# A new hand-written order for an attention and feed-forward kernel, with one small cast moved

## The chip, the cores and the metric

The kernel runs on one core of a Trainium2 chip. The metric is the device time of one launch in microseconds (us), and lower is better. The core's engines work side by side, each through its own queue of instructions in order: PE (TensorE, the matmuls), DVE (VectorE), ACT (ScalarE), POOL (GpSimd) and SP (SyncE, which here only issues DMAs and small waits). PSUM holds matmul results in 8 banks of 512 f32 columns; all other data lie in SBUF.

## The reference

Two branches share the input x (2048 tokens, 640 columns, bf16), and a gate per token mixes them:

```
g = sigmoid((x * gate_w).sum(-1))
q, k, v = x @ wqkv                     # 32 heads of 20 columns
p = softmax(q k^T * 20**-0.5)          # 2048 x 2048 for each head
a = (p v, heads joined) @ wo
h = x @ w1 + b1                        # 1536 columns
b = (h * tanh(softplus(h))) @ w2       # "mish"
out = g * a + (1 - g) * b
```

The bulk of it is the 32 x 2048 x 2048 exponentials, and the score and value matmuls around them.

## The kernel before

**Tiling.** Four heads form a quad (8 of them), and 512 queries a chunk (4 of them); a quad and a chunk make a group, 32 groups G in all. A group has 16 key tiles of 128 keys. A *unit* is the scores of one head, one key tile and one chunk: 128 x 512, one PSUM bank. The four heads of a quad lie 32 rows apart, so up to four score matmuls (L1119), each of 32 rows, can run in PE side by side: a *run* of scores is row-tiled. Everything else on PE is column-tiled: four matmuls of 32 or 21 columns side by side make one *column round*, four value products (L1154, "PV", into the accumulating bank) or one *piece* of a dense product (L699).

**Two ways to the exponential.** Most units go to ACT: one ACTIVATE (L1137) takes one, two or three neighbouring banks and writes into the ring E. The rest, 668 units, go to DVE: L615 (`power_of`) writes the integer whose bits are 2 to the score, into a tile T of four units (one key tile of a group). Such a tile is corrected by POOL: `add_shift` (L645) adds a constant to 64-bit words. `d_take` sets how. With `two` at 0, POOL makes two shifted copies and PV takes the tile in three column rounds. With `two` at 1, POOL makes one copy, DVE adds the two tiles (`total`, L669, 128 x 2048), POOL shifts the other copy, and PV needs two rounds.

**Normalising.** When a group's PV is complete, DVE transposes the bank (L1183), takes reciprocals (L1190) and multiplies by them (L1197, from two SBUF inputs, T1 and rec, into T2), and SP stores the result. L669 and L1197 are the operations with two inputs in SBUF that matter in what follows.

**The dense work.** Every dense product is a *chain* of pieces into one bank and a copy by DVE at its end: keys and queries (`dense_chain`, weights `ws`, stored by way of `st`), values, the hidden product (`h_chain`, weights `w1t`; its copy, L882, adds the bias b1f and writes `big`), its second half (`b_chain`, from `big` and `w2_sb`) and the output product (`wo_chain`; its copy, L998, reads `bl`, a part loaded back from HBM by `load_b`, L965, into one of three slots, which come free when the copies of an earlier `bl` are through). Pieces of the hidden, key and query products are 512 columns wide, those of `b_chain` and `wo_chain` 320. A piece can also be split in four *row parts* (L688), each riding in a run of scores with fewer than four units; SP then issues a small wait (L695) between the parts.

**What sets the order.** The string ORDER, some 6200 tokens, is read from left to right, and each token emits instructions: `S n,bank` n units of scores; `x n` an ACTIVATE over n banks; `D G,j,r,bank` one score unit for DVE, whose L615 waits in a list; `d G,k,two` sets a key tile of group G aside for DVE; `y n` emits the nth waiting DVE operation; `p n,tag` the nth waiting POOL addition; `V j,i` a column round of PV; `C` begins a chain and `F` emits its next piece; `f chain,row` emits one row part. Loads have letters of their own (`l` calls `load_late`). Each engine then runs its share in that order.

**The cast.** The bias b1 is loaded as bf16 (b1bf) by `load_late(2)`. The copy of the very first hidden chain casts it to f32 (L881) just ahead of its own addition.

Of the kernel before, what the change touches and what calls it, by code (L numbers as in the profile page):

```python
# [19 lines left out]
S2,5 x2 S2,2 S2,0 C0,4 C1,5 C2,6 F0 F0 F0 F0 F0 F1 y1 F y3 x2 C3,5 S1,2 y4 S1,3 C4,6 x2 x2 F3 F S1,0 y5 S1,1  # L20
C6,5 F F d1,2,0 F F y2 F d0,0,0 x2 F S1,3 y6 x1 S1,2 S1,4 F F F F x1 C5,6 F6 F6 F6 F F6 F F F F6 F6 x1 F6 C7,0
F6 F6 F6 C8,4 y7 S3,1 x2 F7 F5 F7 F7 y8 y9 F7 F F7 y10 y12 S2,1 x1 y11 S2,5 V1,-1 F F F F C9,3 d1,7,0 V0,-1 F8
F8 F8 y13 F8 F8 x2 F F8 F8 F8 F8 S3,0 F8 F8 F8 F8 x2 F8 F8 F x3 F F y14 F S2,5 V2,-1 x2 V3,-1 S1,0 y15 S1,1
y16 y17 C11,5 S1,2 y18 y19 S2,3 C10,6 x3 V4,-1 F F11 F11 F11 F11 F11 F11 F F F11 F F S1,1 q1 S1,2 V5,-1 x2 F11
F11 y20 v0,0 F11 F11 F11 F11 S1,0 C12,3 x2 S1,4 D0,15,3,6 F11 F11 F11 F11 F11 x1 F11 F F11 x1 F y23 S2,1
D0,15,0,0 y24 d3,4,0 d0,6,0 y25 y26 y27 F y28 x2 D0,15,2,5 S1,4 y29 S1,6 F V6,-1 F x1 y30 x1 l3 y31 S1,0 S1,2
x1 C13,5 F F S1,6 x1 S1,3 D0,14,3,1 S1,4 C14,0 F13 F x1 F F13 F13 F y32 y33 F F F V7,-1 S2,1 D0,15,1,6 y34 F F
F F x2 F F F F D0,14,0,5 S2,3 V8,-1 F F y35 F F F x2 D0,14,1,6 S2,1 y36 F V9,-1 C15,6 y37 y38 y39 x2 V10,-1
S3,3 x2 F F y40 F x3 F y41 l2 F F F F D0,14,2,2 y22 S2,0 y21 p1,8 V15,0 F F V11,-1 S1,5 y42 S1,3 y43 V14,0 y44
D1,15,1,2 x2 S1,4 S1,0 p2,-1 y45 S1,1 x1 p3,-1 C16,5 D1,15,0,6 V12,-1 F F V15,1 F y46 x2 F F l0 x2 F F d2,3,0  # L30
S3,2 D1,15,2,6 F p4,5 V15,2 F y47 F V13,-1 S2,0 x3 D1,14,0,6 V14,2 V14,1 y48 y49 S1,3 y50 y51 C17,5 D1,15,3,2
# [306 lines left out]
def kernel(  # L338
# [1106 lines left out]
```

## Time and profile before

| what | value |
|---|---|
| time, median of 3 runs | 685.02 us (684.34 to 685.22) |
| the profiled execution's own time | 685.2 us |
| its span | 683.4 us, so 1.8 us lie around the span |
| busy: PE, ACT, DVE, POOL | 674.0, 667.9, 603.0, 356.8 us |
| granted TensorE clock | 9 tenths or more in all 40 slices, mean 1.00 from 10 to 674 us |

In the profile, a group of instructions is told by its line, engine, operation and tile; its columns are the summed busy time, the mean duration of one, and the idle time of the engine just ahead of them with what ended it. A row of the timeline has the start, the length, the engine and line, and in brackets how long the engine stood idle before it and for what. Matmuls that overlap have overlapping rows, so on PE the distance between starts says more than the length.

### The profile page before, as it was taken

To read this page: it belongs to the slowest core of one execution; us is meant where nothing else is said; L and a number is where in the kernel's file an instruction comes from. 1 tells how busy PE (TensorE), PEld (TensorE's weight loads), DVE (VectorE), ACT (ScalarE), POOL (GpSimd) and SP (SyncE) were. 2 spreads that over 40 slices of the span, in tenths; PEclk is the share of its full clock that TensorE was granted. 3 is DMA by queue.
4 is the path that set the end of the run, shared out by engine and by line. 5 is a ranking of instruction groups with operands and counts; after the bars stand their busy time and mean duration, and the time that the engine had idled before them with its cause. 6 is when DMAs were issued, how large, how long until landed. Compare 5 with 4: busy or idle time off the path is not lost.

```text
span 683.4 us, 24492 instructions
## 1 busy us (share of the span) xinstructions
PE 674.0 (99%) x10339; PEld 236.7 (35%) x10339; DVE 603.0 (88%) x1037; ACT 667.9 (98%) x695; POOL 356.8 (52%) x349
## 2 busy tenths in 40 slices
PE   8999999999999999999999999999999999999997
PEld 4433332323333443333333223222243333333333
DVE  5688989899999889999889988999998988899896
ACT  6999999999999999999999999999999999999995
POOL 5045555454454535575555545456645655565543
PEclk9999999999999999999999999999999999999999
DMA  7443422214312121112132113321322113162231
GB/s 170 99 100 94 89 49 71 49 34 93 74 25 53 38 48 27 26 39 38 44 92 42 34 58 89 46 70 28 58 55 73 19 30 64 25 82 43 56 86 59
DMA packets 128542, 40.47 MB, mean 59 GB/s; under 512 B 94960, under 2 KB 127872, under 8 KB 128432
## 3 DMA queue, kind: packets, MB, share of 16 engines
q1 hardware_dynamic: 126032, 38.29, 25.5%
q8 instruction: 81, 1.33, 0.8%
q10 hardware_dynamic: 2400, 0.62, 0.4%
q14 instruction: 29, 0.24, 0.1%
HBM read 22.29 MB, written 12.78 MB: 51 GB/s over the span
## 4 chain that ended last, share of the span: by engine, by line
PE 81%; ACT 12%; DVE 3%; issue 3%; DMA 1%; POOL 0%; SPq 0%; DVEq 0%; POOLq 0%; ACTq 0%
PE Sp L699 27%; PE Sp L1119 26%; PE Sp L1154 26%; ACT E L1137 12%; DVE T L615 1%; DMA wf<-in_A_wqkv_dram 1%; PE Sp L688 0%; DVE T L669 0%; DVE st L784 0%; DVE T L1197 0%; POOL T L645 0%; PE Sp L1384 0%; PE Sp L1169 0%; DVE ot L1401 0%; PE Sp L1263 0%
## 5 line engine op out<-in xcount | busy, mean ns | idle before, releaser
L1137 ACT ACTIVATE E<-Sp 128x1024 bf16<-128x1024 f32 (+2 forms) x677 | 635.9, 1090 | 3.5 <-PE Sp L1119 2.7
L645 POOL INT64_ADD T<-T x334 | 347.0, 1050 | 311.7 <-DVE T L615 180.1
L615 DVE TENSOR_SCALAR T<-Sp 128x512 int16<-128x512 f32 x668 | 438.1, 684 | 49.8 <-PE Sp L1119 41.0
L1119 PE MATMUL Sp<-qT,kT 32*128 32x512 bf16 x2048 | 260.9, 383 | 1.9 <-DVE T L615 0.9
L1119 PEld LDWEIGHTS <-kT 32*128 32x128 bf16 x2048 | 69.5, 91 | 234.1 <-issue 229.2
L1154 PE MATMUL Sp<-E,VA 128*21 128x512 bf16 x1380 | 129.5, 382 | 0.0
L1154 PE MATMUL Sp<-T,VD 128*21 128x512 bf16 x1272 | 117.6, 382 | 0.1
L699 PE MATMUL Sp<-w_sb,big 128*32 128x320 bf16 x1508 | 77.1, 302 | 0.3 <-DVE T L615 0.2
L699 PE MATMUL Sp<-xT,w1t 128*32 128x512 bf16 x952 | 75.0, 382 | 0.0
L1154 PEld LDWEIGHTS <-VA 128*21 128x21 bf16 x2048 | 44.8, 90 | 62.8 <-issue 55.5
L1154 PE MATMUL Sp<-T,VA 128*21 128x512 bf16 x668 | 64.1, 382 | 0.0
L699 PE MATMUL Sp<-xT,ws 128*32 128x512 bf16 x720 | 56.6, 382 | 0.3 <-DVE VA L838 0.2
L699 PEld LDWEIGHTS <-big 128*32 128x32 bf16 x1508 | 34.0, 95 | 30.3 <-issue 21.2
L1154 PEld LDWEIGHTS <-VD 128*21 128x21 bf16 x1272 | 31.1, 90 | 36.8 <-issue 29.8
L882 DVE TENSOR_SCALAR big<-Sp,b1f 128x512 bf16<-128x512 f32 x48 | 35.6, 742 | 2.2 <-PE Sp L699 1.8
L699 PE MATMUL Sp<-wv,xT 128*32 128x81 bf16 (+2 forms) x960 | 34.8, 257 | 0.0
L699 PE MATMUL Sp<-wo_sb,od 128*32 128x320 bf16 (+1 forms) x604 | 30.3, 300 | 0.0
L699 PEld LDWEIGHTS <-w1t 128*32 128x32 bf16 x952 | 21.5, 94 | 25.2 <-issue 18.0
L784 DVE CAST st<-Sp 128x512 bf16<-128x512 f32 x36 | 24.4, 684 | 2.8 <-PE Sp L699 2.1
L1183 DVE STREAM_TRANSPOSE T<-Sp 128x512 f32<-128x512 f32 x32 | 22.7, 709 | 2.2 <-PE Sp L1154 2.0
L699 PEld LDWEIGHTS <-xT 128*32 128x32 bf16 x960 | 20.6, 96 | 11.3 <-issue 5.9
L699 PEld LDWEIGHTS <-ws 128*32 128x32 bf16 x720 | 17.1, 95 | 19.1 <-issue 12.5
(82 smaller groups left out, 222.5 us busy)
## 6 DMA issues: line engine op xcount, KB each, us to landing
w1t<-in_B_w_dram SPq DMA_DIRECT2D x24, 320.0 KB
q_dram<-st SPq DMA_DIRECT2D x20, 128.0 KB
b_dram<-bt SPq DMA_DIRECT2D x16, 160.0 KB
bl<-b_dram SPq DMA_DIRECT2D x16, 160.0 KB
qT<-q_dram SPq DMA_DIRECT2D x124, 20.0 KB
o_dram<-T SPq DMA_DIRECT2D x120, 20.0 KB
out_dram<-ot SPq DMA_DIRECT2D x15, 160.0 KB
kT<-k_dram SPq DMA_DIRECT2D x28, 80.0 KB
```

The lines of the kernel that those rows point to most:

```text
L615: nc.vector.tensor_scalar(out=dst.bitcast(I16), in0=src, scalar1=inv_sqrt_dh * LOG2E * 128.0, scalar2=127.0 * 128.0 + (BETA2 if two else B ...
L645: nc.gpsimd.int64_add(dst[:, :].bitcast(I64), src[:, :].bitcast(I64), n * 0x0001000100010001)
L699: nc.tensor.matmul(out_[k : k + 32], lhsT=lhsT[:, k : k + 32], rhs=rhs, tile_position=(0, k), start=start, stop=ch.done(), skip_group_chec ...
L784: nc.vector.tensor_copy(out=res["st"][:, :], in_=ps[:, :])
L882: nc.vector.tensor_scalar(out=big[:, pair_of(c, ft), (ft % 2) * QC : (ft % 2 + 1) * QC], in0=ps[:, :], scalar1=b1f[:, ft : ft + 1], scalar ...
L1119: nc.tensor.matmul(ps_cols, lhsT=kT[p][32 * t_ : 32 * t_ + 32, j * P : (j + 1) * P], rhs=qT[G][32 * t_ : 32 * t_ + 32, :], tile_position=( ...
L1137: nc.scalar.activation(E[:, x : x + n, :], allb[:, k0 : k0 + n, :], ACT.Exp, scale=inv_sqrt_dh,)
L1154: nc.tensor.matmul(acc[32 * t_ : 32 * t_ + DH + 1, :], lhsT=lhsT, rhs=rhs, start=(pv_done[G] == 0), stop=(pv_done[G] == pv_total[G] - 1), ...
L1183: nc.vector.transpose(out=st["T1"][:, :, :].rearrange("p b r -> p (b r)"), in_=acc[:, :])
```

## The change

The whole string ORDER is replaced by another one, and the cast of b1 becomes an operation of its own on the list of waiting DVE operations, entered by `load_late(2)` right after the DMA of b1 is issued. In the new kernel lines move up or down by one: L615 is L616, L645 L646, L669 L670, L699 L700, and from the deleted lines on L1119 is L1118, L1154 L1153, L1197 L1196, L998 L997, L965 L964.

```diff
-S2,5 x2 S2,2 S2,0 C0,4 C1,5 C2,6 F0 F0 F0 F0 F0 F1 y1 F y3 x2 C3,5 S1,2 y4 S1,3 C4,6 x2 x2 F3 F S1,0 y5 S1,1
+S2,0 C1,5 S2,2 S1,6 C0,4 x2 F F C2,0 F0 F0 x2 F0 y1 x1 F1 F S2,1 y3 S1,3 y4 C4,6 C3,5 F F4 S1,0 x1 S1,1 y5
...
             if i == 2:
                 nc.sync.dma_start(b1bf, B_b1.rearrange("(ft p) -> p ft", p=P))
+                dve(lambda: nc.vector.tensor_copy(b1f, b1bf))
             load_w1(i - 2)
...
             def copy():
-                if (ft, c) == (0, 0):
-                    nc.vector.tensor_copy(b1f, b1bf)
                 nc.vector.tensor_scalar(
```

Counted over the whole of the two strings and of what they emit:

| what | before | now |
|---|---|---|
| score units for DVE, tiles set aside, POOL additions | 668, 167, 334 | 668, 167, 334 |
| tiles with `two` at 1 (one DVE sum more, one PV round less each) | 16 | 21 |
| ACTIVATEs of one, two, three banks | 38, 575, 64 | 29, 575, 67 |
| whole pieces F | 1210 | 1209 |
| pieces in row parts: 512 wide, 320 wide | 2, 8 | 6, 5 |
| runs of scores on PE; of them, in two rounds | 640; 14 | 638; 15 |

Three places are shown as the two kernels have them. A number behind a name tells one allocation of a tile from another (T, bl) or one of several tiles (kT0, kT1).

The first is on PE in the hidden product. Before, a score matmul is followed by whole pieces of `w1t`, each four matmuls of 32 columns (two of a first piece are shown):

```order
L1119 LDWEIGHTS kT1_82
L1119 MATMUL Sp_90<-qT2_86,kT1_82 128x512
L699 LDWEIGHTS w1t_2604
L699 MATMUL Sp_90<-xT_68,w1t_2604 32x512
L699 LDWEIGHTS w1t_2604
L699 MATMUL Sp_90<-xT_68,w1t_2604 32x512
```

Now, under the weights of the load at the same place (w1t_2595), one piece is split: a row part (L689) of 128 columns rides behind the scores of its run, and whole pieces follow.

```order
L1118 LDWEIGHTS kT1_82
L1118 MATMUL Sp_90<-qT2_86,kT1_82 128x512
L689 LDWEIGHTS w1t_2595
L689 MATMUL Sp_90<-xT_68,w1t_2595 128x512
L700 LDWEIGHTS w1t_2595
L700 MATMUL Sp_90<-xT_68,w1t_2595 32x512
```

What moved: one piece in this chain is no longer a column round of its own, and its four parts are the fourth matmul of four runs of scores.

The second is on DVE, where the normalising multiplication (L1197, then L1196) of the eighth group stands among the L615. Before:

```order
L615 TENSOR_SCALAR T_3731<-Sp_90 128x512
L615 TENSOR_SCALAR T_3815<-Sp_90 128x512
L1190 RECIPROCAL rec_3918<-T1_3828 128x16
L615 TENSOR_SCALAR T_3731<-Sp_90 128x512
L615 TENSOR_SCALAR T_3815<-Sp_90 128x512
L1197 TENSOR_TENSOR T2_1_89<-T1_3828,rec_3918 128x16x20
L597 TENSOR_SCALAR VD_3312<-VA_69 128x7x84
```

POOL's additions at that place, in its own queue, before:

```order
L645 ISA T_3902<-T_3552 128x1024
L645 ISA T_3989<-T_3731 128x1024
L645 ISA T_4020<-T_3815 128x1024
L645 ISA T_4044<-T_3815 128x1024
L645 ISA T_3731<-T_3731 128x1024
```

DVE now, with the multiplication behind the last two units of tile T_3761:

```order
L616 TENSOR_SCALAR T_3548<-Sp_90 128x512
L616 TENSOR_SCALAR T_3761<-Sp_90 128x512
L616 TENSOR_SCALAR T_3548<-Sp_90 128x512
L616 TENSOR_SCALAR T_3761<-Sp_90 128x512 x2
L1196 TENSOR_TENSOR T2_1_89<-T1_3844,rec_3869 128x16x20
L881 TENSOR_SCALAR big_102<-Sp_90,b1f_73 128x512
```

POOL's additions at that place now:

```order
L646 ISA T_3453<-T_3453 128x1024
L646 ISA T_3922<-T_3548 128x1024
L646 ISA T_3934<-T_3548 128x1024
L646 ISA T_3951<-T_3761 128x1024
L646 ISA T_4049<-T_3761 128x1024
```

What moved: before, one unit of DVE stands between the last unit of T_3731, which addition T_3989 takes, and the multiplication; now two units (the row with x2) stand between the last unit of T_3548, which two additions take one after the other, and the multiplication.

The third is on DVE and SP near the end, at the copies of the output product. DVE before:

```order
L998 SCALAR_TENSOR_TENSOR ot_13250<-Sp_90,g_t_75,bl_13057 128x320
L615 TENSOR_SCALAR T_12968<-Sp_90 128x512
L1206 STREAM_TRANSPOSE O_13310<-T2_0_88 128x512
L998 SCALAR_TENSOR_TENSOR big_102<-Sp_90,g_t_75,bl_13266 128x320
L615 TENSOR_SCALAR T_13260<-Sp_90 128x512
L615 TENSOR_SCALAR T_13073<-Sp_90 128x512
L998 SCALAR_TENSOR_TENSOR big_102<-Sp_90,g_t_75,bl_13266 128x320
L615 TENSOR_SCALAR T_13260<-Sp_90 128x512
L615 TENSOR_SCALAR T_13073<-Sp_90 128x512
L998 SCALAR_TENSOR_TENSOR ot_13405<-Sp_90,g_t_75,bl_13316 128x320
L615 TENSOR_SCALAR T_13260<-Sp_90 128x512
L998 SCALAR_TENSOR_TENSOR big_102<-Sp_90,g_t_75,bl_13294 128x320
```

DVE now:

```order
L997 SCALAR_TENSOR_TENSOR big_102<-Sp_90,g_t_75,bl_13237 128x320
L616 TENSOR_SCALAR T_13221<-Sp_90 128x512
L616 TENSOR_SCALAR T_13105<-Sp_90 128x512
L997 SCALAR_TENSOR_TENSOR big_102<-Sp_90,g_t_75,bl_13237 128x320
L616 TENSOR_SCALAR T_13221<-Sp_90 128x512
L616 TENSOR_SCALAR T_13105<-Sp_90 128x512
L997 SCALAR_TENSOR_TENSOR ot_13373<-Sp_90,g_t_75,bl_13367 128x320
L616 TENSOR_SCALAR T_13221<-Sp_90 128x512
L997 SCALAR_TENSOR_TENSOR big_102<-Sp_90,g_t_75,bl_13395 128x320
```

SP before, the loads of these `bl` among the stores:

```order
L965 DMA bl_13266<-b_dram_95 128x640
L1007 DMA out_0_dram<-ot_13250 128x640
L965 DMA bl_13294<-b_dram_95 128x640
L965 DMA bl_13316<-b_dram_95 128x640
L965 DMA bl_13431<-b_dram_95 128x640
L1007 DMA out_0_dram<-ot_13405 128x640
```

SP now:

```order
L1006 DMA out_0_dram<-ot_13094 128x640
L964 DMA bl_13237<-b_dram_95 128x640
L1006 DMA out_0_dram<-ot_13222 128x640
L964 DMA bl_13367<-b_dram_95 128x640
L964 DMA bl_13395<-b_dram_95 128x640
L964 DMA bl_13435<-b_dram_95 128x640
L1006 DMA out_0_dram<-ot_13373 128x640
```

What moved: now `bl_13367` waits for the second copy that reads `bl_13237`, whose slot it takes, and the third DVE operation after that copy reads it; before, `bl_13316` is issued behind the store of ot_13250, and the ninth DVE operation after that tile's second copy reads it.

598 lines of the change are left out of this document (299 added, 299 removed).

## The prediction

> **What bounds the kernel now.** I read the page's busy time first, then its tenths in 40 slices (PE's and the granted clock's), the chain that ended last, the stretch from 10 to 674 us (its columns: length, then PE, PEld, DVE, ACT and POOL busy, clock, DMA share, GB/s) and the list of waits (total, times, longest).
>
> ```profile
> PE 674.0 (99%) x10339; PEld 236.7 (35%) x10339; DVE 603.0 (88%) x1037; ACT 667.9 (98%) x695; POOL 356.8 (52%) x349
> PE   8999999999999999999999999999999999999997
> PEclk9999999999999999999999999999999999999999
> PE 81%; ACT 12%; DVE 3%; issue 3%; DMA 1%; POOL 0%; SPq 0%; DVEq 0%; POOLq 0%; ACTq 0%
> 10.00:674.00 664.00, 661.86 (x10230) 229.53 (x10224) 593.33 (x1005) 661.55 (x684) 352.30 (x341) 1.00 0.26 57
> PE Sp L1119 <- DVE T L615: 0.9, 3, 0.5
> ACT E L1137 <- PE Sp L1119: 2.7, 8, 1.2
> ```
>
> PE is busy for 661.86 of 664 us at the full granted clock, and 81% of the chain is PE's: the kernel ends when PE's list ends. ACT looks just as full (661.55 us) but holds 12% of the chain. DVE is idle for 683.4 - 603.0 = 80 us. PE's waits on DVE's L615 come to 0.9 us: little time lies in waits, most in the number of matmul rounds.
>
> **What a round on PE costs.** From the timeline (start, length), where nothing waits:
>
> ```profile
> 300.42 0.39 PE L1154 MATMUL Sp<-T,VD 128*21 128x512 bf16 x4
> 300.75 0.39 PE L1119 MATMUL Sp<-qT,kT 32*128 32x512 bf16 x3
> 301.07 0.40 PE L1154 MATMUL Sp<-E,VA 128*21 128x512 bf16 x4
> 301.29 0.39 PE L1154 MATMUL Sp<-T,VD 128*21 128x512 bf16 x4
> ...
> 305.32 0.39 PE L1119 MATMUL Sp<-qT,kT 32*128 32x512 bf16 x3
> 305.64 0.46 PE L699 MATMUL Sp<-w_sb,big 128*32 128x320 bf16 x8
> 305.93 0.39 PE L1154 MATMUL Sp<-T,VD 128*21 128x512 bf16 x4
> ```
>
> By starts: a column round of 512 takes 301.29 - 301.07 = 0.22 us; two pieces of 320 take 0.29, so 0.145 each. From the round at 300.42 over the run of scores to the round at 301.07 there are 0.65 us against 0.22 without the run, so a run costs 0.43. The run has three scores; a fourth matmul in it lies beside them.
>
> **PE's share of the change.** From the table of counts:
> - 5 more tiles take the sum, each with one PV round less: -5 x 0.22 = -1.10.
> - 4 more pieces of 512 ride as row parts: -4 x 0.22 = -0.88. The first place shows one.
> - 3 fewer pieces of 320 do: +3 x 0.145 = +0.43.
> - 2 fewer runs: -2 x 0.43 = -0.86.
> - 1 more run needs a second round: +0.22, taken as one round, since no row shows it apart; between 0 and the 0.43 of a run.
>
> The sum is -2.19 us of PE. Not all of it reaches the end, because some stretches are ACT's. I take the chain's 81%: -1.77; the ends are 0 (ACT fills every gap) and -2.19. A part is safe from waiting in SP's queue only if its nop is on time. PE waited little for it before:
>
> ```profile
> PEld L688 <- SPq L695: 1.3, 3, 0.4
> L695 SPq EVENT_SEMAPHORE  x30: 17/17/17, 106.8 to 619.6; - x30
> ```
>
> The 1.3 us were weight loads' waits, which overlap matmuls; 3 more nops (3 for each piece, 33 against 30) I cost at nothing, with 0.4 as their upper end.
>
> **ACT's share.** The ACTIVATEs by size, and seven in a row:
>
> ```profile
> L1137 ACT ACTIVATE E<-Sp 128x1024 bf16<-128x1024 f32 x575 | 545.7, 1073 | 3.3 <-PE Sp L1119 2.5 <-PE Sp L1154 0.2
> L1137 ACT ACTIVATE E<-Sp 128x1536 bf16<-128x1536 f32 x64 | 96.6, 1510 | 0.2 <-PE Sp L1119 0.2
> L1137 ACT ACTIVATE E<-Sp 128x512 bf16<-128x512 f32 x38 | 22.9, 643 | 0.1
> 196.38 6.53 ACT L1137 ACTIVATE E<-Sp 128x1024 bf16<-128x1024 f32 x7
> ```
>
> Nine singles fewer and three triples more are, by means, -9 x 0.643 + 3 x 1.510 = -1.26 us. But neighbours overlap: seven start (6.53 - 1.07) / 6 = 0.91 us apart, 0.16 less than one lasts. With 0.16 off each: -9 x 0.48 + 3 x 1.35 = -0.3 us, which I take. At that spacing the 575 would need 523 us and were busy for 545.7: ACT has about 22 us of slack in the doubles alone, so its saving adds nothing to PE's; both ends are kept for the rival in which ACT is the bound. [...]
>
> **DVE's share.**
>
> ```profile
> L669 DVE TENSOR_TENSOR T<-T x16: 1154/1216/1702, 72.2 to 624.9; 128x2048 bf16<-128x2048 bf16 x16
> L615 DVE TENSOR_SCALAR T<-Sp 128x512 int16<-128x512 f32 x668 | 438.1, 684 | 49.8 <-PE Sp L1119 41.0 <-POOL T L645 0.7 <-PE Sp L688 0.5
> L881 DVE CAST b1f<-b1bf 128x12 f32<-128x12 bf16 x1 | 0.2, 165 | 0.0
> ```
>
> Five sums more are 5 x 1.216 = 6.1 us of DVE. The 80 us of idle time cover them; of L615's idle 49.8, 41.0 are waits for scores. Without that cover the L615 behind would be late, PE would wait for their banks, and 6.1 would be the upper end. The cast is the same instruction of 0.165 us. It stood ahead of the first bias addition, whose bank it kept for 0.165 us; now it stands among L616 and a cast of VA. If b1's DMA is late there, all of DVE behind it waits, and then PE and ACT for what DVE would have done. I cost the move at 0, since 28 operations of DVE are emitted between that DMA and the cast, some 28 x 0.684 = 19 us, four times the longest transfer of which I quote a row (4.68 us, below); the ends are -0.17 and +4.7.
>
> **Collisions of DVE and POOL.** Two-input operations that began during an addition lasted longer:
>
> ```profile
> L1197 DVE TENSOR_TENSOR T<-T,rec x31: 474/482/1308, 45.4 to 658.0; 128x320 bf16<-128x320 f32 x31
> L1197 DVE TENSOR_TENSOR T<-T,rec 128x320 bf16<-128x320 f32 x31 | 18.3, 591 | 0.1
> 187.03 1.04 POOL L645 INT64_ADD T<-T  x1 [1.56 <-DVE T L615]
> 187.45 0.96 DVE L1197 TENSOR_TENSOR T<-T,rec 128x320 bf16<-128x320 f32 x1
> ...
> 436.23 3.29 POOL L645 INT64_ADD T<-T  x3 [2.23 <-DVE T L615]
> 436.33 1.28 DVE L1197 TENSOR_TENSOR T<-T,rec 128x320 bf16<-128x320 f32 x1
> ...
> 529.56 1.31 DVE L1197 TENSOR_TENSOR T<-T,rec 128x320 bf16<-128x320 f32 x1
> 531.52 0.40 PE L1119 MATMUL Sp<-qT,kT 32*128 32x512 bf16 x3 [0.47 <-DVE T L615]
> 532.03 1.02 ACT L1137 ACTIVATE E<-Sp 128x1024 bf16<-128x1024 f32 x1 [0.19 <-PE Sp L1119]
> 532.12 0.46 PE L699 MATMUL Sp<-w_sb,big 128*32 128x320 bf16 x8 [0.20 <-DVE T L615]
> ```
>
> All 31 multiplications lost 31 x (591 - 482) ns = 3.4 us, and the longest of the sums 1702 - 1216 ns = 0.49. The largest collision reached PE with 0.47 + 0.20 = 0.67 us; the rest of the 0.9 us of waits bounds the others. So taking all away gains some 1.1 us (0.9 and the 0.20), at most 2 with delays that no wait shows. [...]
>
> Does the new order have fewer? At the second place, it has more. Before, one unit stands between addition T_3989's source and the product, which began 0.42 us into it (187.03, 187.45) and lost 0.48. Now two units, 2 x 0.684 = 1.37 us, lie between, with two additions of 1.04 back to back: the product begins close behind the start of the second, as at 436.23, and should lose the 1.28 - 0.48 = 0.8 lost there. Reading all 52 two-input operations of the new order in that way, I find 13 that touch an addition, 8 of them with half a microsecond or more; the same reading of the old order finds 9 such, though the trace has only 5 above 0.45 (four products and the sum of 1702). I take 0 for the net, with -1.1 and +2.7 (4 more of the largest) as ends.
>
> **The last bl.** At the third place, only two units, 1.37 us, stand between the end of the slot's old reader and the copy that needs the new load.
>
> ```profile
> 1.66 4.68 DMA wf<-in_A_wqkv_dram
> L965 SPq DMA_DIRECT2D bl<-b_dram x16: 319/433/570, 265.7 to 671.8; - x16
> ```
>
> From above: the chain's one DMA lasted 4.68 us, so DVE would stand for 4.68 - 1.37 = 3.3 us; from below 0. Issuing alone takes 0.43. I take +0.3: these are 160 KB from a load that the queue is otherwise free for, and what follows are a few units whose banks PE wants only later.
>
> **Sum.** -1.77 + 0.3 + 0 = -1.5 us. The profiled execution, 685.2 (span 683.4 and 1.8 around it), lies 0.2 above the median of 685.02; from the median, 683.5 us.
>
> **Rivals.**
> - *ACT bounds after all.* Then PE's rounds are hidden and ACT's -0.3 to -1.26 is left: 684.7 to 683.8, within 0.2%. For it speaks ACT's 661.55 us, against it the 22 us of slack and 12% of the chain. Chance 0.22. That PE's saving is eaten by gaps elsewhere ends in the same place.
> - *New collisions or a late load cost more than the rounds gain (slower).* The mechanism is the lengthened two-input operation: DVE comes late to a bank, PE waits 0.67 a time. It decides from (1.37 + 1.5) / 0.67 = 4.3 large ones more than before; five more give 683.5 + 3.4 = 686.9. For it: the second place, and 13 sites. Against it: the same reading counts too many in the old order. Chance 0.23, with the late bl (3.0 more: 686.5) in it.
> - *The collisions go.* The order leaves none of weight: 683.5 - 1.1 = 682.4, with 2 us 681.5. Against it stands the second place. Chance 0.15.
> - *The change doesn't do what it says:* as many collisions as before, and the gain is the rounds' alone. That is my forecast's own case, with chance 0.40.
>
> **How the numbers follow.** Within 0.2% (1.37 us), about what a measurement of this kernel can tell, is 683.65 to 686.39. The forecast's own case spreads over 682.8 to 684.3, and 683.5 is just on the faster side: of its 0.40 I give 0.28 to faster and 0.12 to same. With 0.15 of the third rival and 0.03 of the first (its lower end), faster has 0.46. Same has 0.12, 0.19 of the first and 0.01 of the second: 0.32. Slower has 0.22. The range, 681.3 to 687.0, takes in the third rival and most of the second.
>
> **What would show it.** PE's busy time in the middle should fall by about 2 us with 20 matmuls fewer in all, and ACT's idle time grow a little. The L670 rows should count 21, and the sum of L1196 above 482 ns each should be near 3.4 us; at 0.5 the third rival is right, at 7 the second. A wait of L997 for a bl of over 1 us near the end shows the late load, a wait behind the cast of b1 the late b1. The forecast is wrong if PE's waits on L616 pass 3 us, or if PE has fewer rounds and ACT's idle time shrinks to nothing.

## The result, and the profile after

| kernel | median of 6 runs | lowest to highest | ratio to before, 95% interval |
|---|---|---|---|
| before | 684.71 us | 684.20 to 686.14 | |
| after | 689.40 us | 689.19 to 691.56 | 1.0072 (1.0056 to 1.0087) |

The new order is slower by 0.7%, some 4.7 us by the medians and 4.9 by the ratio. One of the five executions of *slot* (an experiment below) took 723.83 us at a mean granted clock of 0.85, and no time or ratio here counts it. The profiled execution of after is its longest, 691.56 us; what it has above the others lies almost wholly in one place near the start (the first load of queries, below): by the first sum, at 75.3 us, it is already 2.4 us behind *l3*, the next kernel named, and it is 2.4 us behind at the last sum too. Where a typical execution of the new order is meant, I therefore read the profile of the kernel of the first experiment, *l3* (689.04 us), which differs from after only at that place.

The page of after: busy time, then the chain that ended last.

```profile
PE 675.7 (98%) x10319; PEld 237.4 (34%) x10319; DVE 608.4 (88%) x1042; ACT 667.4 (97%) x689; POOL 357.7 (52%) x349
PE 78%; ACT 10%; DVE 6%; issue 3%; DMA 1%; POOL 1%; SPq 0%; DVEq 0%; ACTq 0%; POOLq 0%
```

PE has the 20 matmuls fewer, yet is not busy for less (674.1 us in *l3*, 674.0 before), and DVE's share of the chain went from 3% to 6%. The stretch from 10 us to some 9.5 us before the end (length, then PE, PEld, DVE, ACT and POOL busy, clock, DMA share, GB/s), of after and of *l3*:

```profile
10.00:680.00 670.00, 662.44 (x10195) 229.63 (x10191) 598.78 (x1010) 660.32 (x677) 352.32 (x339) 1.00 0.27 56
```

```profile
10.00:677.70 667.70, 662.03 (x10215) 229.77 (x10205) 599.07 (x1011) 661.16 (x678) 352.62 (x341) 1.00 0.26 56
```

PE stands idle there for 670.00 - 662.44 = 7.6 us in after and 5.7 us in *l3*, against 664.00 - 661.86 = 2.1 us before. So of the 3.7 us by which this stretch of *l3* is longer than before, 3.5 are PE standing still, and not more work. The waits in after that grew (total, times, longest):

```profile
ACT E L1136 <- PE Sp L1118: 9.8, 14, 2.2
PE Sp L1118 <- DVE T L616: 1.3, 3, 0.8
PEld L1118 <- DMA qT<-q_dram: 1.7, 1, 1.7
```

The first row stood at 2.7 before, and it is 6.4 in *l3*: ACT now waits for scores that PE brings late. PE is late for DVE, for one load of queries (qT), and, by way of DVE, for one load of `bl` (DVE's wait of 1.37 us at L997, shown below). The operations of DVE that lasted longer where a POOL addition ran, before and after (the normalising multiplication, then the scaling of VA into VD, L597 and now L598, which has one input in SBUF):

```profile
L597 DVE TENSOR_SCALAR VD<-VA 128x588 bf16<-128x588 bf16 x16 | 6.1, 386 | 0.0
L597 DVE TENSOR_SCALAR VD<-VA x16: 320/326/585, 33.3 to 451.0; 128x588 bf16<-128x588 bf16 x16
```

```profile
L1196 DVE TENSOR_TENSOR T<-T,rec 128x320 bf16<-128x320 f32 x31 | 18.4, 594 | 0.2
L598 DVE TENSOR_SCALAR VD<-VA 128x588 bf16<-128x588 bf16 x16 | 7.9, 499 | 0.0
L598 DVE TENSOR_SCALAR VD<-VA x16: 315/324/1168, 33.0 to 455.2; 128x588 bf16<-128x588 bf16 x16
L670 DVE TENSOR_TENSOR T<-T x21: 1203/1215/2053, 75.3 to 629.8; 128x2048 bf16<-128x2048 bf16 x21
```

The multiplications lose 31 x (594 - 482) ns = 3.5 us (3.4 before), the longest sum 0.84 (0.49 before): hardly more than before. The scalings lose 16 x (499 - 324) ns = 2.8 us against 16 x (386 - 326) ns = 1.0 us, and the longest takes 1.17 us in place of 0.32. Two places in after where this reaches PE and ACT:

```profile
98.21 5.35 POOL L646 INT64_ADD T<-T  x5 [2.54 <-DVE T L616]
98.63 0.81 DVE L598 TENSOR_SCALAR VD<-VA 128x588 bf16<-128x588 bf16 x1
99.36 1.27 DVE L1196 TENSOR_TENSOR T<-T,rec 128x320 bf16<-128x320 f32 x1
101.88 0.39 PE L1118 MATMUL Sp<-qT,kT 32*128 32x512 bf16 x2 [0.79 <-DVE T L616]
102.66 1.02 ACT L1136 ACTIVATE E<-Sp 128x1024 bf16<-128x1024 f32 x1 [1.21 <-PE Sp L1118]
...
400.24 2.14 POOL L646 INT64_ADD T<-T  x2 [3.49 <-PE Sp L1153]
400.35 1.17 DVE L598 TENSOR_SCALAR VD<-VA 128x588 bf16<-128x588 bf16 x1
402.16 0.37 PE L1118 MATMUL Sp<-qT,kT 32*128 32x512 bf16 x1 [0.27 <-DVE T L616]
403.75 1.02 ACT L1136 ACTIVATE E<-Sp 128x1024 bf16<-128x1024 f32 x1 [0.42 <-PE Sp L1118]
```

At 98.63 a scaling begins in the first of five additions (5.35 us, so 1.07 each: the first ends at about 99.28) and ends at 99.44; the multiplication right behind it ends at 100.63, the second addition at about 100.35: DVE loses 0.49 + 0.79 us in a row, PE then stands 0.79 us for a bank and ACT 1.21 us for scores.

### The profile page after: what moved, and what is told of

The parts are those of the page before. It is cut to its first block, busy times and chain, and to the rows that moved or that the text cites. A ratio compares the mean times of both kernels' runs of the same rounds, so it can differ in the third digit from the quotient of the medians.

```text
span 689.7 us, 24457 instructions
## 1 busy us (share of the span) xinstructions
PE 675.7 (98%) x10319; PEld 237.4 (34%) x10319; DVE 608.4 (88%) x1042; ACT 667.4 (97%) x689; POOL 357.7 (52%) x349
## 4 chain that ended last, share of the span: by engine, by line
PE 78%; ACT 10%; DVE 6%; issue 3%; DMA 1%; POOL 1%; SPq 0%; DVEq 0%; ACTq 0%; POOLq 0%
PE Sp L700 26%; PE Sp L1118 25%; PE Sp L1153 25%; ACT E L1136 10%; DVE T L616 3%; POOL T L646 1%; DVE st L785 1%; DVE T L1196 1%; DVE VD L598 0%; PE Sp L1383 0%; DMA w1t<-in_B_w_dram 0%; DMA qT<-q_dram 0%; PE Sp L545 0%; DMA bl<-b_dram 0%; PE Sp L689 0%
## 5 line engine op out<-in xcount | busy, mean ns | idle before, releaser
L646 POOL INT64_ADD T<-T x334 | 347.8, 1051 | 317.7 <-DVE T L616 168.4
L616 DVE TENSOR_SCALAR T<-Sp 128x512 int16<-128x512 f32 x668 | 435.6, 682 | 48.4 <-PE Sp L1118 39.9
L1118 PE MATMUL Sp<-qT,kT 32*128 32x512 bf16 x2048 | 262.4, 384 | 4.2 <-DMA qT<-q_dram 1.4
L1118 PEld LDWEIGHTS <-kT 32*128 32x128 bf16 x2048 | 69.6, 91 | 236.7 <-issue 230.9
L1153 PE MATMUL Sp<-E,VA 128*21 128x512 bf16 x1380 | 129.4, 383 | 0.0
L1153 PE MATMUL Sp<-T,VD 128*21 128x512 bf16 x1252 | 116.5, 383 | 1.2 <-POOL T L646 0.9
L700 PE MATMUL Sp<-w_sb,big 128*32 128x320 bf16 x1520 | 78.6, 302 | 0.2 <-DVE T L616 0.2
L700 PE MATMUL Sp<-xT,w1t 128*32 128x512 bf16 x940 | 74.1, 383 | 0.0
L1153 PEld LDWEIGHTS <-VA 128*21 128x21 bf16 x2048 | 45.1, 90 | 60.6 <-issue 52.7
L1153 PE MATMUL Sp<-T,VA 128*21 128x512 bf16 x668 | 63.7, 382 | 0.0
L700 PE MATMUL Sp<-xT,ws 128*32 128x512 bf16 x716 | 57.2, 382 | 0.4 <-DVE T L616 0.3
L1153 PEld LDWEIGHTS <-VD 128*21 128x21 bf16 x1252 | 30.9, 90 | 42.7 <-issue 35.3
L700 PEld LDWEIGHTS <-big 128*32 128x32 bf16 x1520 | 34.7, 95 | 29.5 <-issue 21.5
L700 PE MATMUL Sp<-wv,xT 128*32 128x81 bf16 (+2 forms) x960 | 37.1, 260 | 1.0 <-issue 0.6
L700 PE MATMUL Sp<-wo_sb,od 128*32 128x320 bf16 (+1 forms) x604 | 29.2, 300 | 0.9 <-DVE ot L997 0.9
L700 PEld LDWEIGHTS <-w1t 128*32 128x32 bf16 x940 | 20.8, 94 | 25.9 <-issue 19.2
L670 DVE TENSOR_TENSOR T<-T 128x2048 bf16<-128x2048 bf16 x21 | 26.5, 1260 | 0.0
L700 PEld LDWEIGHTS <-xT 128*32 128x32 bf16 x960 | 21.7, 98 | 12.8 <-issue 6.7
```

Source lines behind the costliest of these rows:

```text
L616: nc.vector.tensor_scalar(out=dst.bitcast(I16), in0=src, scalar1=inv_sqrt_dh * LOG2E * 128.0, scalar2=127.0 * 128.0 + (BETA2 if two else B ...
L646: nc.gpsimd.int64_add(dst[:, :].bitcast(I64), src[:, :].bitcast(I64), n * 0x0001000100010001)
L670: nc.vector.tensor_tensor(out=d[0][:, :], in0=d[0][:, :], in1=d["T"][:, :], op=ALU.add)
L700: nc.tensor.matmul(out_[k : k + 32], lhsT=lhsT[:, k : k + 32], rhs=rhs, tile_position=(0, k), start=start, stop=ch.done(), skip_group_chec ...
L1118: nc.tensor.matmul(ps_cols, lhsT=kT[p][32 * t_ : 32 * t_ + 32, j * P : (j + 1) * P], rhs=qT[G][32 * t_ : 32 * t_ + 32, :], tile_position=( ...
L1153: nc.tensor.matmul(acc[32 * t_ : 32 * t_ + DH + 1, :], lhsT=lhsT, rhs=rhs, start=(pv_done[G] == 0), stop=(pv_done[G] == pv_total[G] - 1), ...
```

## The experiments

The theory after the result: the new order loses at places where DVE is late (held scalings, held multiplications, the late `bl`), and these can be taken away one by one by moving tokens. The rival: the loss is spread, through more work on DVE (five sums more) or the pieces that ride as row parts, and no single place holds it. All runs are compared by their ratio to before on the same chip. The interval of a ratio is 0.0012 to 0.0016 to each side for after and its single edits, and about 0.0009 for the kernels near before. The "gain" of an edit of after is read against 1.0060 (*l3*) and 1.0072 (after) alike; as the difference of two ratios it is uncertain by some 1.2 us, so a gain below that is not shown by the times alone.

**The load of weights ahead of the load of queries (l3).**

```diff
-C12,6 S1,3 l3 D0,15,3,0 ... y27 q1 y28
+C12,6 S1,3 D0,15,3,0 ... y27 q1 l3 y28
```

> The changed kernel (689.4 us) with one token moved: the second late load of w1 (320 KB) is issued behind the first load of qT and no longer ahead of it. Theory of the late loads: SP spent 1.73 us on that w1 load at 32.05 and PE then stood 1.39 us (1.77 with what followed) for qT at 36.79; about -1.8 us, so 687.6, and no stretch of the clock at 0.5 behind it. Theory of the collisions alone: PE loses nothing there that it doesn't lose elsewhere, 689.4 within 0.5.

Measured: 689.14 us, 1.0060 (1.0048 to 1.0072). In after, SP issues a load of `w1t` (L474) ahead of qT (L813); before, qT was issued at 30.44 and `w1t` behind it, at 34.79. The issue of qT before, the timeline of after, and the microseconds behind it:

```profile
30.44 1.41 SPq L812 DMA_DIRECT2D qT<-q_dram  x4
```

```profile
32.05 1.73 SPq L474 DMA_DIRECT2D w1t<-in_B_w_dram  x1
33.89 1.50 SPq L813 DMA_DIRECT2D qT<-q_dram  x4
36.79 1.18 PE L1118 MATMUL Sp<-qT,kT 32*128 32x512 bf16 x5 [1.39 <-DMA qT<-q_dram]
```

```profile
35.00:36.00 1.00, 0.40 (x5) 0.09 (x1) 0.00 (x0) 0.62 (x2) 0.80 (x1) 1.00 1.03 309
36.00:37.00 1.00, 0.21 (x2) 0.13 (x5) 0.00 (x0) 0.00 (x0) 0.90 (x2) 0.77 0.66 214
37.00:38.00 1.00, 1.00 (x9) 0.17 (x11) 0.42 (x1) 0.20 (x1) 0.37 (x1) 0.50 0.54 102
38.00:39.00 1.00, 1.00 (x16) 0.43 (x17) 0.87 (x2) 1.00 (x2) 0.00 (x0) 0.50 0.80 36
39.00:40.00 1.00, 1.00 (x28) 0.74 (x20) 0.00 (x0) 0.74 (x1) 0.00 (x0) 0.53 1.09 336
```

PE stands 1.4 us for qT, and then gets half the clock for some 3 us (the third number from the end of each row). Behind qT the load of weights does no harm: *l3* has no such wait. But the median moved by only 0.3 us, not by the 1.8 expected, so this stall makes a few executions long, and is not why the order is slow: five of the six runs of after lie between 689.19 and 689.86 without the edit. The other profiled executions agree by their mean granted clock, 0.997 in that of after: of the edits below that leave this load where it was, only *pv* is below 0.999 there (0.998, in its longest, 691.46 us); *slot*, *scale*, *mult*, *mult2* and *whole* (687.2 to 689.8 us) have 0.999 or 1.00.

**The late bl (slot).** The slot that came free last is given out first; this edit takes the one that has been free for longest.

```diff
-        bl_tag[s] = bl_slots.pop()
+        bl_tag[s] = bl_slots.pop(0)
```

> The changed kernel with the slots of bl taken in the order in which they came free (the oldest first) and not the newest first: bl_13367 then takes a slot that has long been free. Theory of the late loads: DVE's wait of 1.37 us for bl at 671.7 goes, and with it PE's 0.86 to 1.03 at 672.3; about -1.0 us, 688.4. Rival: the tail has its own limit (ACT and the stores at the end), and nothing changes, 689.4.

Measured: 687.72 us, 1.0044 (1.0031 to 1.0057): a gain of 1.1 to 1.9 us. It is the least certain one, since one of the four executions took 689.46 us, as long as after; that the wait is gone, the trace shows. The end of the kernel in after, then in *slot*:

```profile
668.54 0.54 DVE L997 SCALAR_TENSOR_TENSOR big<-Sp,g_t,bl 128x320 bf16<-128x320 f32 x1
669.10 2.05 SPq L964 DMA_DIRECT2D bl<-b_dram  x3
671.73 0.55 DVE L997 SCALAR_TENSOR_TENSOR ot<-Sp,g_t,bl 128x320 bf16<-128x320 f32 x1 [1.37 <-DMA bl<-b_dram]
672.33 0.73 PE L700 MATMUL Sp<-wo_sb,od 128*32 128x320 bf16 x16 [0.86 <-DVE ot L997]
673.52 1.94 ACT L1136 ACTIVATE E<-Sp 128x1024 bf16<-128x1024 f32 x2 [0.75 <-PE Sp L1118]
```

```profile
663.71 2.77 SPq L964 DMA_DIRECT2D bl<-b_dram  x2
667.72 0.55 DVE L997 SCALAR_TENSOR_TENSOR ot<-Sp,g_t,bl 128x320 bf16<-128x320 f32 x1 [0.31 <-PE Sp L700]
```

In after the load starts at 669.10, when its slot's last reader is through, and is used at 671.73, so it takes 2.6 us. DVE stands 1.37 us, PE 0.86 and ACT 0.75. In *slot* the copy waits for PE alone.

**The scalings (scale).** Six scalings of VA are emitted where no addition runs; one of the six moves:

```diff
-S1,2 y140 ... x2 y142 y128 D3,10,1,2
+S1,2 y128 y140 ... x2 y142 D3,10,1,2
```

> The changed kernel with six of the 16 scalings of VD (L598, one input) moved by a few tokens to where POOL adds nothing. In its trace these six lasted 468 to 1168 ns against 324. Theory that L598 collides with POOL as the two-input operations do: DVE gets back 2.8 us, L598 is 0.32 everywhere, and PE loses its 0.50 at 139.8, its 0.65 at 402.2 and half of its 1.17 at 101.9: about -1.7 us, 687.7. Rival, that only operations with two inputs count and L598 was long for another reason: it stays long or the time stays, 689.4.

Measured: 687.77 us, 1.0041 (1.0029 to 1.0053): a gain of 1.3 to 2.1 us. The scalings' loss went to nothing (mean 499 to 316 ns), while the multiplications lost 0.6 us more, since one met an addition anew (1.29 us at 133.83):

```profile
L1196 DVE TENSOR_TENSOR T<-T,rec 128x320 bf16<-128x320 f32 x31 | 19.0, 614 | 0.2
L598 DVE TENSOR_SCALAR VD<-VA 128x588 bf16<-128x588 bf16 x16 | 4.8, 316 | 0.0
```

**The multiplications (mult, mult2).** *mult* moves eight of them out of additions; two of its moves:

```diff
-d8,0,0 F y242 F ... y266 y267
+d8,0,0 F F ... y266 y242 y267
-D20,13,3,5 y648 D20,12,0,4 ... d20,0,0 y653
+D20,13,3,5 D20,12,0,4 ... d20,0,0 y648 y653
```

> The changed kernel with eight of the 31 normalising multiplications (L1196) moved to where POOL adds nothing; in its trace they lasted 598 to 1274 ns against 481. Theory of the collisions: DVE gets back 3.4 us, PE loses its 0.53 at 310 and half of its 1.17 at 101.9: about -1.2 us, 688.2. Rival, that these collisions are covered by DVE's idle time: below 0.4 us, 689.4.

Measured: 689.19 us, 1.0068 (1.0052 to 1.0083): no gain, though the multiplications' mean fell from 594 to 485 ns. A later multiplication makes its four stores later, and here they stood ahead of a load of queries in SP's queue:

```profile
440.08 1.93 SPq L1229 DMA_DIRECT2D o_dram<-T  x4
442.06 3.73 SPq L813 DMA_DIRECT2D qT<-q_dram  x8
446.53 0.39 PE L1118 MATMUL Sp<-qT,kT 32*128 32x512 bf16 x3 [0.40 <-DMA qT<-q_dram]
```

So the run mixes two effects, hits taken away and a load made late. *mult2* differs from it in two tokens: it leaves y648 where it was, and takes y121, which *mult* had moved ahead, further on instead:

```diff
-p32,3 D4,14,0,1 y121 S2,5 ... D4,13,1,6 y150
+p32,3 D4,14,0,1 S2,5 ... D4,13,1,6 y121 y150
```

> The changed kernel with seven multiplications moved, without the one whose four stores, issued later, held up a load of qT in e4_mult (PE waited 0.78 us at 446), and with the one at 99 us moved 43 tokens later, not ahead of a copy that PE waited for. If the multiplications' collisions cost time by themselves: -1.0 us, ratio 1.0057. Rival, that they are covered: 1.0068 to 1.0072 as in e4_mult.

Measured: 687.53 us, 1.0036 (1.0023 to 1.0049): a gain of 1.6 to 2.5 us, the largest of all single edits, with the scalings as held as in after (mean 499 ns). Which of the two tokens makes the 1.7 us between *mult* and *mult2* was not tried.

```profile
L1196 DVE TENSOR_TENSOR T<-T,rec 128x320 bf16<-128x320 f32 x31 | 15.1, 488 | 0.2
```

**A value product ahead of POOL (pv).** At 488.94 in after, PE stands for the corrected tile of POOL, whose five additions follow one another:

```profile
483.84 6.06 POOL L646 INT64_ADD T<-T  x5 [0.56 <-PE Sp L1153]
488.94 0.40 PE L1153 MATMUL Sp<-T,VD 128*21 128x512 bf16 x4 [0.85 <-POOL T L646]
```

```diff
-V12,0 y719 y721 S2,2 V11,0 V11,2 x2 d22,5,0 ... V7,-1 V13,1
+V12,0 y719 y721 S2,2 V11,0 x2 d22,5,0 ... V7,-1 V11,2 V13,1
```

> The changed kernel (ratio 1.0072) with one PV round, which waited 0.85 to 1.03 us for POOL at 486 to 489, moved nine tokens back, behind the scores and three PV rounds. If a wait of PE counts in full: -1.0 us, ratio 1.0057. Rival, that ACT, which waited 0.85 us there for scores, has slack enough: 1.0072.

Measured: 689.05 us, 1.0064 (1.0049 to 1.0079). That wait is gone (the round now stands sixteen tokens later), and the time moved by 0.5 us at most: within the interval of nothing, and not the 1.0 us of the wait.

**The cast alone, in the kernel before (cast).**

```diff
-e0 S2,3 V14,2 y67
+e0 S2,3 V14,2 B y67
...
-                if (ft, c) == (0, 0):
-                    nc.vector.tensor_copy(b1f, b1bf)
...
+        "B": lambda: nc.vector.tensor_copy(b1f, b1bf),
```

> The kernel before with only the cast of b1 made early: 28 vector operations behind the issue of its DMA, as in the changed kernel. All theories: 0.16 us of DVE in another place, and b1 has long landed; 685.0 within 0.4 us. If the cast's new place is a cause of the loss: up to 4 us slower.

Measured: 685.20 us, 0.9999 (0.9989 to 1.0008). It costs and gains nothing.

**Clearing the kernel before (clear, clear2).** *clear* moves five scalings and five multiplications of the old order out of additions; one of each:

```diff
-V7,-1 x2 F y141 y102 F ... V11,1 y144 V9,-1
+V7,-1 x2 F y141 F ... V11,1 y102 y144 V9,-1
-v3,0 S1,4 y227 S1,5 ... q8 x1 y231
+v3,0 S1,4 S1,5 ... q8 x1 y227 y231
```

> The kernel before with five of its scalings of VD (L597) and five of its normalising multiplications (L1197) moved to where POOL adds nothing; its trace has 1.0 and 3.2 us of DVE lost there. Theory of the collisions: DVE gets back 4.2 us, and PE the 0.67 at 531.5, the 0.18 at 438 and what else came late: about -1.3 us, 683.7. Rival, that DVE's idle time covers them: 685.0.

Measured: 683.86 us, 0.9981 (0.9972 to 0.9990).

```profile
L1197 DVE TENSOR_TENSOR T<-T,rec 128x320 bf16<-128x320 f32 x31 | 15.1, 487 | 0.1
L597 DVE TENSOR_SCALAR VD<-VA 128x588 bf16<-128x588 bf16 x16 | 5.5, 356 | 0.0
```

One scaling is hit anew (0.81 us at 187.33, inside the addition that began at 186.91; 0.32 before). *clear2* moves it too, and lets one POOL addition go ahead of another beside the longest sum:

```diff
-D8,13,3,0 S1,3 x1 S1,5 y230 y279 ... S1,4 y289 y290
+D8,13,3,0 S1,3 x1 S1,5 y279 ... S1,4 y289 y230 y290
-F p98,-1 F73 ... F81 p101,-1 F81
+F F73 F76 C85,0 y343 F77 F80 y342 p101,-1 p98,-1 F ... F81 F81
```

> The kernel before with the ten operations moved as in e6_clear (ratio 0.9981 there), and three tokens more: the scaling that began to meet an addition at 187 in that run (809 ns) goes elsewhere, and two POOL additions change places, so that the sum at 233 (1702 ns) meets none. DVE gets back another 1.0 us; by 0.4 to 0.65 us for one us of DVE (the prices of e6_clear and e3_scale), 0.4 to 0.6 us less than e6_clear: ratio 0.9972 to 0.9976. Rival, that what is left is covered: 0.9981.

Measured: 683.38 us, 0.9977 (0.9969 to 0.9986), which can't be told from *clear*'s 0.9981. The scaling is free now, but the exchange of the additions missed: the longest sum still lasts 1.70 us.

```profile
L669 DVE TENSOR_TENSOR T<-T x16: 1154/1215/1700, 72.5 to 624.0; 128x2048 bf16<-128x2048 bf16 x16
```

This is the fastest kernel of the study, faster than both before and after. So held scalings and multiplications cost the old order some 1.3 to 1.6 us. The prediction's price for an order without collisions (1.1, at most 2) has the same size, but it counted the sum, which is still held here, and not the scalings.

**More hits in the kernel before (hit).** The reverse: seven scalings are moved into additions; two of them:

```diff
-F F y135 y168 ... F S1,0 y202
+F F y168 ... F S1,0 y135 y202
-y576 y548 x2 ... p193,0 y610
+y576 x2 ... p193,0 y548 y610
```

> The reverse: the kernel before, with seven of its scalings of VD moved to places where DVE reaches them just behind the start of a POOL addition (0.92 to 1.02 us of it left in the trace of before). If the scaling is blocked until the addition ends, each lasts 1.2 us in place of 0.32, DVE loses some 5.6 us, and at 0.4 to 0.65 us for one the kernel takes 2.2 to 3.6 us more: ratio 1.0032 to 1.0053. Rival, that the scalings were long in the changed kernel for another reason: 0.32 each, ratio 1.0000.

Measured: 685.16 us, 1.0002 (0.9993 to 1.0010). Four of the seven met an addition (0.81 to 1.18 us), so the edit did less than was meant: the mean is 551 ns, 16 x (551 - 326) ns = 3.6 us lost, 2.6 more than before and in all more than in after. By the expected 0.4 to 0.65 us for one that would still be 1.0 to 1.7 us; the time moved by 0.7 us at most. Two of the hits:

```profile
136.61 1.04 POOL L645 INT64_ADD T<-T  x1 [1.60 <-PE Sp L1119]
136.73 1.11 DVE L597 TENSOR_SCALAR VD<-VA 128x588 bf16<-128x588 bf16 x1
138.48 0.39 PE L1119 MATMUL Sp<-qT,kT 32*128 32x512 bf16 x2 [0.18 <-DVE T L615]
...
425.14 1.18 DVE L597 TENSOR_SCALAR VD<-VA 128x588 bf16<-128x588 bf16 x1
426.24 0.73 DVE L882 TENSOR_SCALAR big<-Sp,b1f 128x512 bf16<-128x512 f32 x1
427.02 0.83 PE L699 MATMUL Sp<-xT,w1t 128*32 128x512 bf16 x12 [0.36 <-DVE big L882]
```

A hit of 0.8 us brought PE 0.18 us of waiting at one place and 0.36 at the other; at the pair of hits around 99 us of after, 1.28 us brought 0.79. Before, PE has no such wait at the first two places. DVE's lost time is thus not a price: what a hit brings to PE differs from place to place. That it is what is left after the slack that DVE has there is how I read these rows; no run varied the slack.

**Whole pieces in place of row parts (whole, new_whole, old_whole).** Ten pieces (five of 512, five of 320 columns) of the new order are made whole again, priced by the prediction's rounds at 5 x 0.22 + 5 x 0.145 = 1.8 us.

```diff
-f24,2 y89 ... p16,-1 V1,-1 S1,3 f24,3 ... f24,1 ... f24,0
+y89 ... p16,-1 F24 V1,-1 S1,3
```

> The changed kernel with ten of its eleven pieces in row parts (five of 512, five of 320) made whole column rounds again. By the prices of the sum, 5 x 0.22 + 5 x 0.145 = 1.8 us of PE more, 1.5 with the chain's 81%: about 690.8. Rival, that ACT or DVE sets the pace and PE's rounds are covered: 689.2 within 0.4.

Measured: 689.91 us, 1.0068 (1.0054 to 1.0081), so 0.5 us above after by the medians, and not above it by the ratios. In the new order cleared (the next experiment but one) and the old order cleared (*clear2*, two pieces of 512 and eight of 320, priced at 1.6 us) the same was done:

> e8_all with ten of its eleven pieces in row parts made whole again: by the prices of the sum 1.8 us more PE. In the changed kernel as it was this cost about 0.5 us. If the waits had hidden the rounds there, it costs 1.4 us or more here, ratio 1.0020; if rounds are in general worth a third of their price, 1.0007.

> e9_clear2 with all ten of its pieces in row parts made whole again: 2 x 0.22 + 8 x 0.145 = 1.6 us more PE. At the full price ratio 1.0000, at a third 0.9985.

Measured: 686.10 us, 1.0017 (1.0008 to 1.0026), and 684.13 us, 0.9994 (0.9985 to 1.0002): 1.2 us more than the cleared kernel each, by the ratios (1.0 and 0.75 by medians). In the cleared orders a piece that rides is thus worth about six tenths of its price, uncertain by half the price. In after nothing was measured, but the interval there, some 1.2 us, doesn't exclude the same 1.2 us. The five PV rounds and the two runs fewer, the larger part of the prediction's sum, were not tried by themselves.

**The sums (new_nosum, old_nosum).** Both leave out most of the computation of L670 and L669: the sum of two tiles runs over the first 8 of 2048 columns only. They stand on the cleared new and the cleared old order.

```diff
-            nc.vector.tensor_tensor(out=d[0][:, :], in0=d[0][:, :], in1=d["T"][:, :], op=ALU.add)
+            nc.vector.tensor_tensor(out=d[0][:, 0:8], in0=d[0][:, 0:8], in1=d["T"][:, 0:8], op=ALU.add)
```

> e8_all, the new order with its found waits removed (ratio 0.9999), with each of the 21 sums over 8 columns in place of 2048: it leaves out most of the sum of two tiles, so that 21 x 1.1 = 23 us of DVE are free. To be read against e14_old_nosum. If the five sums more are what keeps the cleared new order 1.7 us behind the cleared old one (0.9977), the gap closes by over 1 us here. If the order of PE and ACT holds it: the gap stays between 1.2 and 2.2 us, with both a little faster.

> e9_clear2, the old order with its collisions moved (ratio 0.9977), with each of its 16 sums over 8 columns in place of 2048: it leaves out most of the sum. Some 17.6 us of DVE are free. If DVE's load costs time at all, 0.5 to 2 us less; if not, 0.9977.

Measured: 684.80 us, 0.9999 (0.9990 to 1.0008), and 683.90 us, 0.9983 (0.9974 to 0.9992). DVE's busy time fell to 583.4 and 585.1 us, and no time was gained in either, within some 0.9 us. In the cleared orders the five sums more are covered, so the rival that the extra work on DVE makes the new order slow falls there; after itself, where DVE is late at places, was not run without them.

**Everything repaired (all).** After with *l3*, *slot*, *pv*, the six scalings, eight multiplications (the seven of *mult2* and y196, which *scale* had brought into an addition) and one pair of POOL additions exchanged (p100 ahead of p98).

> The changed kernel with the late w1 load, the slots and the six scalings as before, seven multiplications moved (without the one whose stores came ahead of a load of qT), one PV round moved a few tokens later, where PE waited 1.03 us for POOL at 486, and one POOL addition issued ahead of the one that met the sum at 233. If the waits add up: 689.2 - 0.3 (w1) - 1.4 (slot) - 1.5 (scalings) - 1.2 (multiplications) - 1.0 (PV) - 0.5 (sum) = 683.3, below the kernel before. Rival, that a freed wait comes back at the next late thing: 686 or more.

Measured: 685.09 us, 0.9999 (0.9990 to 1.0008), 4.2 to 5.0 us below after, where the waits added up to 5.9. The longest sum is free here (2.05 us in after, at most 1.36 now). The same stretch as above in *all*, then in *clear2*:

```profile
10.00:673.80 663.80, 660.93 (x10199) 229.58 (x10196) 593.02 (x1011) 659.90 (x677) 349.66 (x339) 1.00 0.27 57
```

```profile
10.00:673.00 663.00, 661.05 (x10214) 228.83 (x10210) 589.25 (x1005) 660.28 (x684) 349.80 (x339) 1.00 0.27 57
```

PE's idle time is down to 2.9 us (5.7 in *l3*). What the places named above cost is thereby shown in sum. But the repaired new order is not faster than before, and the repaired old order is, by 1.6 us: against that 1.6, the places account for some 3 of the 4.7 us between before and after, and not for the rest. The three pairs of the two cleared orders (*all* and *clear2*, the two without sums, the two with whole pieces) differ by 1.5, 1.1 and 1.6 us, each uncertain by some 0.9. The two profiled executions lie only 0.6 us apart, since that of *clear2* (684.40 us) is its longest; PE's idle time in them differs by 0.9 us (2.87 against 1.95), its busy time by 0.1. This remainder is open: no experiment separated its cause, though the difference is there with and without the sums, and with the pieces whole, so neither makes all of it. A row of PE is 0.39 us long while the next round can start 0.22 us behind it (the rounds at 301.07 and 301.29 before), so lateness of up to 0.17 us a time shows in no row as waiting; whether the remainder is made of such lateness was not tried.

## Why the prediction was wrong

Forecast 683.5 us in 681.3 to 687.0, measured 689.4. Of the rivals, the second had the direction, and its late `bl` came true, but the time went past its 686.5 to 686.9. Its mechanism, more lengthened two-input operations, did not come: the prediction's own sign for it was a sum of 7 us over the multiplications, and 3.5 were measured. What was held more, and was not in the prediction, are the scalings with one input.

- *"I take the chain's 81%: -1.77": the saving did not arrive.* The counts were right (20 matmuls fewer, 21 sums). But with the held operations out of both orders, where the new one should have been 1.77 us faster, it is 1.1 to 1.6 slower. The pieces that ride bring about 0.6 of their price in these orders; the PV rounds (-1.10) and the runs (-0.86) were not tried, and why their part does not arrive is open. PE's busy time in the middle, forecast to fall by 2 us, rose by 0.2 in *l3* and fell by 0.9 in *all*; but it fell by 0.8 in *clear2* too, which has all the rounds of before, so it does not count rounds. A chain that is 81% PE's says that PE's work set the end, and not that every round taken away arrives there.
- *"I take 0 for the net" (collisions): the net was right, the list too short, and the price wrong.* The two-input operations lost 3.5 + 0.84 = 4.3 us where 3.4 + 0.49 = 3.9 were lost before; the multiplications' sum came out at 3.5 where 3.4 was forecast. The second place went the other way, though: its product should have begun at the start of the second addition and lasted 1.28 us (0.8 lost), but DVE had waited 0.60 us for scores ahead of it, and it began late in that addition and lost 0.2 (0.48 before). Of the 13 two-input operations that the reading had touching an addition, 8 by half a microsecond or more, the trace of after has some 10 held and 4 by that much. That the net came out is therefore partly luck: the reading gave neither how many nor which.

```profile
191.32 3.30 POOL L646 INT64_ADD T<-T  x3 [0.83 <-DVE T L616]
192.42 0.69 DVE L616 TENSOR_SCALAR T<-Sp 128x512 int16<-128x512 f32 x1 [0.60 <-PE Sp L1118]
193.03 0.68 DVE L1196 TENSOR_TENSOR T<-T,rec 128x320 bf16<-128x320 f32 x1
```

And only operations with two inputs in SBUF were read. The scalings with one were left out, although one of the old trace's had lasted 0.59 against 0.33 us. They lost 1.8 us more than before, and moving them gained 1.3 to 2.1. This is the step that failed in the term for the collisions: 0 was forecast, and what was measured is some 2.1 us (added up below).
- *"So taking all away gains some 1.1 us": the right size for the old order, partly by luck (*clear2*), and no price for the new.* Clearing the old order gained 1.3 to 1.6. In the new order the same kind of clearing gained 1.3 to 2.1 (scalings, 2.9 us of DVE) and 1.6 to 2.5 (multiplications, 3.3 us), while in *hit* 2.6 us more of held time cost at most 0.7. A price per hit was carried from one order to another, although it belongs to the place.
- *"I take +0.3" (the last bl): mis-sized.* The mechanism was named and its bounds, 0 to 3.3, hold the measured 1.1 to 1.9. Its sign, a wait of L997 of over 1 us, came: DVE waited 1.37 us; the load took 2.6 us from the issue to the copy's start, longer than the 1.37 us of cover. "A few units whose banks PE wants only later" was the false step: PE stood 0.86 us behind it.
- *SP's queue: overlooked.* The prediction followed SP at the third place alone. The load of weights that now stands ahead of the first queries is in the order of both kernels and was not read. It costs 0.3 us at the median and some 2.4 in the profiled execution.
- *Right:* the cast at 0 (*cast*), the five sums covered by DVE's idle time (the two kernels without sums, cleared orders both), and that ACT does not bound: with 687.2 - 667.6 = 19.6 us in *l3* against 15.5 before, it stands idle longer. The nops, costed at 0, were not tried by themselves; the weight loads' waits for them went from 1.3 to 2.4 us.
- *What would have shown it wrong* was "PE's waits on L616 pass 3 us". They came to 2.3 us (1.3 at L1118, 1.0 at L700), while PE's idle time grew by 3.5: a sign that looked at one releaser was too narrow.

Added up, by the middles of the gains: scalings 1.7 and multiplications 2.0, less the 1.6 that such hits cost before, make 2.1; `bl` makes 1.5. That is 3.6 of the 4.7 us, of which *all* shows some 3 together. The difference of the cleared orders, 1.1 to 1.6, is the rest, and it is open. More is open than it shows: if the 2.19 us of rounds are worth 0.6 of their price, 1.3 us, the new order loses some 2.4 to 2.9 us at places that are not named here. The parts are each uncertain by some 1.2 us.

## What to carry to other kernels

Before pricing an order by its collisions, list every DVE operation that has stretched rows in the trace, whatever its inputs, and look at each in its place: how late DVE already is there and who waits for it next, not only how many nanoseconds it loses. An operation that is moved takes its stores and loads along in SP's queue; both the load that now stands behind and the slot that now comes free late are read from the same order. And a repair is worth making on the old kernel too: here the search for why the new order was slow found 0.2% in the old one. And after an edit, look whether it did what it was meant to: in *hit* three of seven moves met nothing, and in *clear2* the sum stayed held.

## What the runs showed of the hardware

- A scaling from SBUF to SBUF in bf16 (128 x 588, one tensor input) took 0.32 us alone and up to 1.18 us (425.14 in *hit*) where it began inside a 64-bit addition of POOL, and at the places read here it ended some 0.2 us behind that addition. At 136.73 in *hit* it began 0.12 us into an addition of 1.04 us and lasted 1.11: the addition ends at 136.61 + 1.04 = 137.65 and the scaling at 137.84, 0.19 us later, where a whole scaling takes 0.32. At 400.35 in after it began 0.11 us into the first of two additions (2.14 us, so 1.07 each) and lasted 1.17; at 187.33 in *clear* some 0.2 us lie between the two ends as well. L616, whose one input lies in PSUM, was held nowhere in after: its 668 rows last 624 to 693 ns.
- The granted clock was 1.00 from 10 to 36 us in after, 0.77 from 36 to 37, 0.50, 0.50 and 0.53 in the three microseconds behind, and 1.00 again from 40. PE had waited 1.39 us until 36.79; it was busy for 0.40 of the microsecond before and 0.21 of the one in which the clock fell. *l3*, without that wait, has 1.00 from 36 to 40, and after itself has a mean of 1.00 from 60 to 680 us, although PE waits there too, for up to 0.9 us at a time. How long a wait has to be, and when the clock falls behind it, was not tried.
